# Top-32 attention and MLP-mixer: VectorE operations recast so that none reads two SBUF tiles in the tile loop, and the candidate chain interleaved

## The chip, the cores and the metric

The kernel runs on one core of one Trainium2 chip. The metric is the device time of one launch in microseconds; the median of the runs is compared. A profile is one execution recorded by the hardware profiler. In what follows VectorE is DVE in the profile's rows, ScalarE is ACT, GpSimd is POOL, TensorE is PE (its weight loads PEld), SyncE is SP.

## The reference

Attention over 8 batches and 8 heads, sequence 576, head width 64, where each query row keeps its 32 largest scores; the heads are concatenated and go through an MLP-mixer with a residual. In short:

```python
scores = scale * np.matmul(q, k.transpose(0, 1, 3, 2))          # 576 x 576 for each of 64 heads
kth = np.partition(scores, -32, axis=-1)[..., -32:-31]          # 32nd largest of each row
scores = np.where(scores >= kth, scores, -1e9)
attn = np.exp(scores - max); attn /= attn.sum + 1e-9
x = (attn @ v), heads side by side                              # 8 x 576 x 512
h = np.maximum(x.transpose(0, 2, 1) @ w_tok1, 0) @ w_tok2       # token mixing, 256 wide
u = x + h.transpose(0, 2, 1)
out = u + np.maximum(u @ w_ch1, 0) @ w_ch2                      # channel mixing, 1536 wide
```

## The kernel before

Two heads of one batch make a pair; there are 32 pairs. A pair's scores are cut into nine tiles of 128 query rows by 576 keys (four of each head, and one that holds the last 64 rows of both), 288 tiles in all. The loop bodies don't emit instructions: they add operations to a plan, each with an engine, an assumed duration and a due time (T is the assumed period of a tile), the operations it depends on, and the buffers it takes and uses. Plan.run then lists the operations engine by engine: at each step it takes the operation that could start first, and among those within 0.12 us of each other the one with the earlier due time. The instructions are emitted in that order, and each engine runs its own in that order.

A tile goes through these steps (tile_ops):

- TensorE multiplies q and k in float32 into PSUM, two tiles at a time (mm, L367; L359 for the ninth), in two of three "big" slots that the transposes of q and k and the MLP also use; ScalarE copies the scores into an Ssb buffer (L444) and takes exp of them into E, bfloat16 (L446).
- VectorE looks for a threshold near the 32nd largest score. The row's 576 scores are cut into seven segments and MAX8 gives each one's eight largest (L451), 56 candidates cd. Then MAX8 over the first two of each segment (L458); cut: scores at or above the eighth are set to zero by a scalar_tensor_tensor that reads cd twice (L461); MAX8 over the first five of each segment (L468); cut again (L461); MAX8 over all (L470), whose eighth value is th, of rank 24 to 31.
- ScalarE takes the sign of th - score (L472), bfloat16, and its row sum cnt, which tells th's rank. GpSimd multiplies scores and signs into X (L476), so that scores above the threshold become negative, and writes behind them seven dummies that are huge or hugely negative by cnt (L478). VectorE's MAX8 over X's 583 columns (L483) then has the 32nd largest score in place eight: m.
- VectorE writes the mask M = score >= m (L485); GpSimd multiplies E by M into Pm (L488) and copies th and m into thi and tlo for a test at the end (L491, L492).
- SyncE issues a DMA transpose of Pm into PT (L493). When a pair's nine are there, TensorE multiplies them by v and a column of ones (pv, L397), and VectorE divides by the sum on the way out of PSUM into Xb (L417 to L429).

When the four pairs of a batch are done, mlp_ops puts 33 groups of matmuls into the plan (TensorE L515 to L574, ScalarE L521 to L582), due over the next 36 tiles, and five stores. Behind the last tile VectorE tests that all thresholds were found (L604 to L619); a fallback that computes everything anew runs only if one wasn't.

Of the kernel before, what the change touches and what calls it, by code (L numbers as in the profile page):

```python
# [16 lines left out]
NDUM = 7  # L17


class Buf:  # L20
# [10 lines left out]
class Plan:  # L31
# [29 lines left out]
    def run(self):  # L61
# [15 lines left out]
        n = len(self.ops)  # L77
        while len(order) < n:
            best = None
            for eng, cs in cand.items():  # L80
                t0 = free[eng]
                pick = None
                early = None
                for o in cs:
                    r = o.ready if o.ready > o.due - self.AHEAD else o.due - self.AHEAD
                    ok = all(b.t is not None or b in o.acq for b in o.use)
                    taken = {}
                    for b in o.acq:
# [12 lines left out]
                    if early is None or r < early[0]:  # L101
                        early = key
                    if pick is None:
                        pick = (key, o)
                    else:
                        pr = pick[0][0]
                        if abs(r - pr) < 0.12:
                            if (o.due, o.n) < pick[0][1:]:
                                pick = (key, o)
                        elif r < pr:  # L110
                            pick = (key, o)
                if pick is not None and (best is None or pick[0][0] < best[0][0]):
                    best = pick
# [17 lines left out]
            done = o.end + o.lat  # L131
            if o.dma:
                dma_free = max(dma_free, o.end) + o.dma
                done = max(done, dma_free + 1.8)
# [6 lines left out]
                    s[1], s[2] = b.end, True  # L141
            for c in o.kids:
                c.wait -= 1
                t = done if (c.eng != o.eng or o.dma) else o.end
                if t > c.ready:
                    c.ready = t
                if c.wait == 0:
                    cand[c.eng].append(c)
# [7 lines left out]
def kernel(  # L156
# [23 lines left out]
    scale = 1.0 / float(D) ** 0.5  # L180
# [3 lines left out]
    ST = S - SM  # L184
    NPAIR = B * H // 2
    NT = NPAIR * 9
    XW = S + NDUM
    bounds = [round(i * S / NSEG) for i in range(NSEG + 1)]

    main = ExitStack()  # L190
# [3 lines left out]
    def sbt(name, shape, dt):  # L194
        return sb.tile(shape, dt, name=name, tag=name)
# [13 lines left out]
    kdum = sbt("kdum", [P, NDUM], f32)  # L209
    w1b = sbt("w1b", [P, 5, DT], bf16)  # L210
    w2b = sbt("w2b", [P, NJ, S], bf16)
    wc1b = sbt("wc1b", [P, NC, DC], bf16)
    wc2b = sbt("wc2b", [P, NF, C], bf16)
    cnt = sbt("cnt", [P, NT], f32)
    thi = sbt("thi", [P, NT], f32)
    tlo = sbt("tlo", [P, NT], f32)

    qLs = slots("qL", 3, [P, 5, 2, D], f32)
    slots("kL", 3, [P, 5, 2, D], f32)
    slots("vL", 2, [P, 5, 2, D], f32)  # L220
# [216 lines left out]

    def tile_ops(i, s, S_, om):

        E, cd, m8, th = Buf("E"), Buf("cd"), Buf("m8"), Buf("th")  # L440
        sg, X, M, Pm, PT = Buf("sg"), Buf("X"), Buf("M"), Buf("Pm"), Buf("PT")
        t = T * i

        ev = plan.add("ACT", 0.6, t + 0.6 * T, lambda: nc.scalar.copy(out=S_.t[:, :], in_=s.t[:, 0:S]),  # L444
                      [om], use=[s, S_])
        ex = plan.add("ACT", 0.6, t + 2.0 * T, lambda: nc.scalar.activation(  # L446
            out=E.t[:, :], in_=S_.t[:, :], func=AF.Exp, scale=scale), [ev], acq=[E], use=[S_])
        last = None
# [23 lines left out]
        ct = plan.add("ACT", 0.78, t + 2.2 * T, lambda: nc.scalar.activation(  # L472
            out=sg.t[:, :], in_=S_.t[:, :], func=AF.Sign, scale=-CUT, bias=th.t[:, 7:8],
            accum_out=cnt[:, i : i + 1]), [a5], acq=[sg], use=[S_, th])

        xm = plan.add("POOL", 1.4, t + 2.7 * T, lambda: nc.gpsimd.tensor_tensor(  # L476
            out=X.t[:, 0:S], in0=S_.t[:, :], in1=sg.t[:, :], op=ALU.mult), [ct], acq=[X], use=[S_, sg])
# [114 lines left out]
    for o in order:  # L592
# [204 lines left out]
```

## Time and profile before

| | |
|---|---|
| median of 2 runs | 1442.6 us (1441.63 to 1443.57) |
| the profiled execution's own time | 1438.56 us |
| its span | 1436.8 us |
| busy in the span: VectorE | 1281.4 us (89%) |
| TensorE matmul / weight loads | 893.9 us (62%) / 484.8 us (34%) |
| GpSimd | 907.7 us (63%) |
| ScalarE | 735.7 us (51%) |
| mean granted TensorE clock | 0.73 |

Busy time is the union of an engine's instructions over the span; the mean duration of one instruction stands in the groups of instructions; the timeline gives the start of each, in microseconds from the span's start, and merges neighbours of one kind (x7 is seven instructions, the time that of all). An engine's idle time before an instruction, and what ended it, stands behind it in brackets.

### The profile page before, as it was taken

What the parts mean: (1) busy time and instruction counts of PE and PEld (TensorE: products, weight loads), DVE (VectorE), ACT (ScalarE), POOL (GpSimd) and SP (SyncE); (2) the same over time, 40 slices, a digit from 0 to 9 for tenths busy, and PEclk for the clock granted to TensorE, in tenths of its full rate; (3) what the DMA queues carried; (4) which work ended last, traced back from release to release, by engine and by line L of the source; (5) the groups of instructions that cost most, each with busy time, mean ns of one, the idle gap of its engine ahead of it and who ended that gap; (6) DMA issues with size and microseconds to landing.
All of it is one profiled execution on the core that took longest, in us unless ns stands there. A gap on an engine that the chain in (4) does not pass through costs nothing. (4 is left out here: it accounts for less than half of the span.)

```text
span 1436.8 us, 18917 instructions
## 1 busy us (share of the span) xinstructions
PE 893.9 (62%) x4797; PEld 484.8 (34%) x4850; DVE 1281.4 (89%) x4256; ACT 735.7 (51%) x1465; POOL 907.7 (63%) x1451
## 2 busy tenths in 40 slices
PE   3645555875587665776567755687557656577437
PEld 2322323432343332433233322343224323333214
DVE  2999999999989999899999999899998999999960
ACT  2544446654466454654556544665446554565413
POOL 1756667666666666766676666766666666666640
PEclk9998557885578655976579855797558865698559
DMA  9422223332222322333223322333223332122111
GB/s 170 107 58 51 47 57 62 63 90 59 44 58 61 88 62 56 63 61 68 61 62 61 83 51 52 62 68 85 62 49 58 68 73 45 33 38 66 36 32 36
DMA packets 317190, 90.02 MB, mean 63 GB/s; under 512 B 309968, under 2 KB 311824, under 8 KB 317072
## 3 DMA queue, kind: packets, MB, share of 16 engines
q1 hardware_dynamic: 314496, 84.99, 28.8%
q0 software_dynamic: 2576, 3.74, 1.5%
q8 instruction: 40, 0.66, 0.2%
q14 instruction: 78, 0.64, 0.2%
HBM read 35.78 MB, written 9.44 MB: 31 GB/s over the span
## 5 line engine op out<-in xcount | busy, mean ns | idle before, releaser
L476 POOL TENSOR_TENSOR X<-Ssb,sg 128x576 f32<-128x576 f32 x288 | 369.2, 1282 | 268.9 <-DVE cd L451 135.5
L472 ACT ACTIVATE sg<-Ssb,th 128x576 bf16<-128x576 f32 x288 | 223.1, 775 | 577.3 <-DVE th L470 354.3
L488 POOL TENSOR_TENSOR Pm<-E,M 128x576 bf16<-128x576 bf16 x288 | 366.8, 1273 | 182.3 <-issue 163.5
L461 DVE SCALAR_TENSOR_TENSOR cd<-cd,m 128x14 f32<-128x14 f32 (+1 forms) x576 | 385.5, 669 | 19.6
L451 DVE MAX8 cd<-Ssb 128x8 f32<-128x82 f32 (+1 forms) x2016 | 321.7, 228 | 51.7 <-ACT Ssb L444 51.7
L367 PE MATMUL big<-kT,qT 64*128 64x512 f32 (+1 forms) x1024 | 303.4, 597 | 97.2 <-ACT Ssb L444 72.7
L397 PE MATMUL one<-vb,PT 128*128 128x65 bf16 (+2 forms) x1600 | 153.5, 228 | 221.6 <-DMA PT<-Pm 190.7
L367 PEld LDWEIGHTS big<-kT,qT 64*128 64x128 f32 x1024 | 148.9, 252 | 241.3 <-ACT Ssb L444 108.1
L483 DVE MAX8 m<-X 128x8 f32<-128x583 f32 x288 | 216.2, 751 | 3.6 <-POOL X L478 3.6
L485 DVE TENSOR_SCALAR M<-Ssb,m 128x576 bf16<-128x576 f32 x288 | 209.5, 728 | 8.6
L397 PEld LDWEIGHTS <-PT 128*128 128x128 bf16 (+2 forms) x1600 | 104.6, 113 | 269.7 <-DMA PT<-Pm 195.7
L446 ACT ACTIVATE E<-Ssb 128x576 bf16<-128x576 f32 x288 | 184.7, 682 | 1.7
L444 ACT COPY Ssb<-big 128x576 f32<-128x576 f32 x288 | 171.6, 630 | 9.4 <-PE big L367 5.0
L554 PE MATMUL big<-UT,wc1b 128*128 128x64 bf16 (+1 forms) x745 | 122.0, 316 | 79.8 <-ACT H L560 34.2
L569 PE MATMUL one<-wc2b,H 128*128 128x512 bf16 (+1 forms) x465 | 128.4, 422 | 21.8 <-DVE Xb L418 11.4
L478 POOL TENSOR_SCALAR X<-kdum,cnt 128x7 f32<-128x7 f32 x288 | 97.9, 340 | 27.4
L554 PEld LDWEIGHTS <-wc1b 128*128 128x128 bf16 x768 | 59.7, 107 | 140.8 <-issue 103.9
L569 PEld LDWEIGHTS <-H 128*128 128x128 bf16 (+1 forms) x480 | 50.6, 110 | 81.9 <-issue 33.6
L470 DVE MAX8 th<-cd 128x8 f32<-128x56 f32 x288 | 63.2, 220 | 9.7
L560 ACT ACTIVATE H<-big 128x576 bf16<-128x576 f32 x96 | 60.3, 643 | 18.3 <-PE big L554 17.9
L359 PE MATMUL big<-kT,qT 128*128 128x64 f32 (+1 forms) x128 | 59.2, 602 | 12.3 <-ACT kT L337 12.2
L468 DVE MAX8 m<-cd 128x8 f32<-128x35 f32 x288 | 57.1, 198 | 9.8
(67 smaller groups left out, 704.1 us busy)
## 6 DMA issues: line engine op xcount, KB each, us to landing
qL<-in_q_dram SPq DMA_DIRECT2D x64, 128.0 KB, 2.9
kL<-in_k_dram SPq DMA_DIRECT2D x64, 128.0 KB, 2.8
vL<-in_v_dram SPq DMA_DIRECT2D x64, 128.0 KB, 2.8
out_dram<-ob SPq DMA_DIRECT2D x32, 256.0 KB, 2.0
PT<-Pm SPq DMA_TRANSPOSE x288, 2.6
wc1b<-in_moe_w_ch_dram POOLq DMA_DIRECT2D x1, 1536.0 KB, 13.3
wc2b<-in_moe_w_ch_dram POOLq DMA_DIRECT2D x1, 1536.0 KB, 22.9
qL<-in_q_dram SPq DMA_DIRECT2D x64, 16.0 KB, 2.5
```

Source lines behind the costliest of these rows:

```text
L367: nc.tensor.matmul(out=bs[h].t[:, lo:hi], lhsT=qT.t[r, g * P : (g + 1) * P], rhs=kT.t[r, lo:hi], start=True, stop=True,)
L397: nc.tensor.matmul(out=o[0:m, g, :], lhsT=src[0:kr, j, cs], rhs=vb.t[0:kr, j, h, :], start=(j == 0), stop=(j == 4),)
L446: ex = plan.add("ACT", 0.6, t + 2.0 * T, lambda: nc.scalar.activation(out=E.t[:, :], in_=S_.t[:, :], func=AF.Exp, scale=scale), [ev], acq= ...
L451: segs.append(plan.add("DVE", 0.155, t + T + 0.01 * a, lambda a=a: nc.vector.max(cd.t[:, a, :], S_.t[:, bounds[a] : bounds[a + 1]]), [ev], ...
L461: return lambda: nc.vector.scalar_tensor_tensor(out=cd.t[:, :, 0:n], in0=cd.t[:, :, 0:n], scalar=m8.t[:, 7:8], in1=cd.t[:, :, 0:n], op0=AL ...
L472: ct = plan.add("ACT", 0.78, t + 2.2 * T, lambda: nc.scalar.activation(out=sg.t[:, :], in_=S_.t[:, :], func=AF.Sign, scale=-CUT, bias=th.t ...
L476: xm = plan.add("POOL", 1.4, t + 2.7 * T, lambda: nc.gpsimd.tensor_tensor(out=X.t[:, 0:S], in0=S_.t[:, :], in1=sg.t[:, :], op=ALU.mult), [ ...
L483: m = plan.add("DVE", 0.7, t + 3.4 * T, lambda: nc.vector.max(mx.t[:, :], X.t[:, 0:XW]), [dm], acq=[mx], use=[X])
L485: mk = plan.add("DVE", 0.4, t + 3.6 * T, lambda: nc.vector.tensor_scalar(out=M.t[:, :], in0=S_.t[:, :], scalar1=mx.t[:, 7:8], scalar2=None ...
L488: pm = plan.add("POOL", 1.4, t + 3.9 * T, lambda: nc.gpsimd.tensor_tensor(out=Pm.t[:, 0:S], in0=E.t[:, :], in1=M.t[:, :], op=ALU.mult), [m ...
L554: nc.tensor.matmul(out=pb.t[:, lo:hi], lhsT=wc1b[:, cc, fc * P : (fc + 1) * P], rhs=UT.t[:, cc, lo:hi], start=(cc == 0), stop=(cc == NC - 1))
L569: nc.tensor.matmul(out=pb.t[0:r, 0:C], lhsT=H2.t[:, fc, cs], rhs=wc2b[:, fc, :], start=(fc == 0), stop=False)
```

## The change

- The two cuts become match_replace: the eight values that MAX8 found are replaced by -1e30 in cd. Its operands are cd and the eight values.
- th and m are written straight into thi and tlo, which are now eight wide for each tile; GpSimd's two copies go.
- The dummies move from GpSimd to VectorE (a tensor_scalar of 3 rows of 3 columns at a pitch of 4, so nine dummies, in X's columns 576 to 587; the pad columns are set to a hugely negative value once). The long MAX8 reads 588 columns.
- The mask product has three forms, by the tile's place among nine. In six of nine ScalarE's exp goes into a "big" slot of PSUM, in float32, ordered behind X; VectorE does mask and product in one scalar_tensor_tensor that reads scores from SBUF and exp from PSUM. In two of nine VectorE negates the threshold (nt), and GpSimd makes the mask by two passes with one input (a huge multiple of the difference, clamped to 0 and 1) and multiplies. In one of nine GpSimd compares in one pass and multiplies.
- The plan: a VectorE result is ready for VectorE only 0.11 us after its operation; candidates for a start count as equal within 0.03 us in place of 0.12; the segments of a tile don't depend on each other any more; assumed durations and T (3.1 for 2.95) are new. Slots: kL 2 for 3, Ssb 8 for 6, PT 18 for 20, nt 4, Z 2, no th.

The diff, cut to its core:

```diff
@@ Plan.run
-                        if abs(r - pr) < 0.12:
+                        if abs(r - pr) < 0.03:
...
-                t = done if (c.eng != o.eng or o.dma) else o.end
+                t = done if (c.eng != o.eng or o.dma) else o.end + (0.11 if o.eng == "DVE" else 0.0)
@@ buffers
-    thi = sbt("thi", [P, NT], f32)
-    tlo = sbt("tlo", [P, NT], f32)
+    thi = sbt("thi", [P, NT, 8], f32)
+    tlo = sbt("tlo", [P, NT, 8], f32)
...
-    slots("kL", 3, [P, 5, 2, D], f32)
+    slots("kL", 2, [P, 5, 2, D], f32)
...
-    slots("Ssb", 6, [P, S], f32)
+    slots("Ssb", 8, [P, S], f32)
...
-    slots("PT", 20, [P, 5, P], bf16)
+    slots("PT", 18, [P, 5, P], bf16)
...
     for j in range(NDUM):
-        nc.vector.memset(kdum[:, j : j + 1], float(2 * (j + 1) - 529))
+        nc.vector.memset(kdum[:, j // 3, j % 3 : j % 3 + 1], float(2 * (j + 1) - 529))
+    for t in Xs:
+        nc.vector.memset(t[:, S:XW], -BIG)
...
-    T = 2.95
+    T = 3.1
@@ tile_ops
-        ex = plan.add("ACT", 0.6, t + 2.0 * T, lambda: nc.scalar.activation(
-            out=E.t[:, :], in_=S_.t[:, :], func=AF.Exp, scale=scale), [ev], acq=[E], use=[S_])
...
-            if a:
-                segs[a].deps.append(segs[a - 1])
...
         def cut(n):
-            return lambda: nc.vector.scalar_tensor_tensor(
-                out=cd.t[:, :, 0:n], in0=cd.t[:, :, 0:n], scalar=m8.t[:, 7:8], in1=cd.t[:, :, 0:n],
-                op0=ALU.is_lt, op1=ALU.mult)
+            return lambda: nc.vector.match_replace(cd.t[:, :, 0:n], m8.t[:, :], cd.t[:, :, 0:n], NEG)
...
-        a5 = plan.add("DVE", 0.14, tr + .04, lambda: nc.vector.max(th.t[:, :], cd.t[:, :, :]), [a4], acq=[th], use=[cd])
+        a5 = plan.add("DVE", 0.125, tr + .04, lambda: nc.vector.max(thi[:, i, :], cd.t[:, :, :]), [a4], use=[cd])
...
-        dm = plan.add("POOL", 0.15, t + 2.71 * T, lambda: nc.gpsimd.tensor_scalar(
-            out=X.t[:, S:XW], in0=kdum[:, :], scalar1=cnt[:, i : i + 1], scalar2=-BIG,
-            op0=ALU.add, op1=ALU.mult), [xm], use=[X])
-        mx = Buf("m8")
-
-        m = plan.add("DVE", 0.7, t + 3.4 * T, lambda: nc.vector.max(mx.t[:, :], X.t[:, 0:XW]), [dm], acq=[mx], use=[X])
-
-        mk = plan.add("DVE", 0.4, t + 3.6 * T, lambda: nc.vector.tensor_scalar(
-            out=M.t[:, :], in0=S_.t[:, :], scalar1=mx.t[:, 7:8], scalar2=None, op0=ALU.is_ge),
-            [m], acq=[M], use=[S_, mx])
-        pm = plan.add("POOL", 1.4, t + 3.9 * T, lambda: nc.gpsimd.tensor_tensor(
-            out=Pm.t[:, 0:S], in0=E.t[:, :], in1=M.t[:, :], op=ALU.mult), [mk, ex], acq=[Pm], use=[E, M])
-        kp = plan.add("POOL", 0.25, t + 3.95 * T, lambda: (
-            nc.gpsimd.tensor_copy(out=thi[:, i : i + 1], in_=th.t[:, 7:8]),
-            nc.gpsimd.tensor_copy(out=tlo[:, i : i + 1], in_=mx.t[:, 7:8])), [m], use=[th, mx])
+        dm = plan.add("DVE", 0.09, t + 3.3 * T, lambda: nc.vector.tensor_scalar(
+            out=X.t[:, S:XW].rearrange("p (a b) -> p a b", a=3)[:, :, 0:3], in0=kdum[:, :, 0:3],
+            scalar1=cnt[:, i : i + 1], scalar2=-BIG, op0=ALU.add, op1=ALU.mult), [ct, xm], use=[X])
+
+        m = plan.add("DVE", 0.68, t + 3.4 * T, lambda: nc.vector.max(tlo[:, i, :], X.t[:, 0:XW]), [dm, xm], use=[X])
+        thr = tlo[:, i, 7:8]
+        form = (0, 0, 1, 0, 0, 2, 0, 0, 1)[i % 9]
+        if form == 0:
+            Ep = Buf("big")
+            ex = plan.add("ACT", 0.6, t + 3.2 * T, lambda: nc.scalar.activation(
+                out=Ep.t[:, 0:S], in_=S_.t[:, :], func=AF.Exp, scale=scale), [ev, xm], acq=[Ep], use=[S_])
+            pm = plan.add("DVE", 0.7, t + 3.6 * T, lambda: nc.vector.scalar_tensor_tensor(
+                out=Pm.t[:, 0:S], in0=S_.t[:, :], scalar=thr, in1=Ep.t[:, 0:S], op0=ALU.is_ge, op1=ALU.mult),
+                [m, ex], acq=[Pm], use=[S_, Ep])
+        else:
+            ex = plan.add("ACT", 0.6, t + 2.4 * T, lambda: nc.scalar.activation(
+                out=E.t[:, :], in_=S_.t[:, :], func=AF.Exp, scale=scale), [ev], acq=[E], use=[S_])
+            if form == 1:
+                nt, Z = Buf("nt"), Buf("Z")
+                tn = plan.add("DVE", 0.07, t + 3.5 * T, lambda: nc.vector.tensor_scalar(
+                    out=nt.t[:, :], in0=thr, scalar1=-(1.0 - 2.0**-24), scalar2=None, op0=ALU.mult),
+                    [m], acq=[nt])
+                z = plan.add("POOL", 0.8, t + 3.7 * T, lambda: nc.gpsimd.tensor_scalar(
+                    out=Z.t[:, :], in0=S_.t[:, :], scalar1=nt.t[:, :], scalar2=BIG, op0=ALU.add, op1=ALU.mult),
+                    [tn], acq=[Z], use=[S_, nt])
+                mk = plan.add("POOL", 0.8, t + 3.71 * T, lambda: nc.gpsimd.tensor_scalar(
+                    out=M.t[:, :], in0=Z.t[:, :], scalar1=1.0, scalar2=0.0, op0=ALU.min, op1=ALU.max),
+                    [z], acq=[M], use=[Z])
+            else:
+                mk = plan.add("POOL", 2.0, t + 3.7 * T, lambda: nc.gpsimd.tensor_scalar(
+                    out=M.t[:, :], in0=S_.t[:, :], scalar1=thr, scalar2=None, op0=ALU.is_ge),
+                    [m], acq=[M], use=[S_])
+            pm = plan.add("POOL", 1.31, t + 3.9 * T, lambda: nc.gpsimd.tensor_tensor(
+                out=Pm.t[:, 0:S], in0=E.t[:, :], in1=M.t[:, :], op=ALU.mult), [mk, ex], acq=[Pm], use=[E, M])
```

## Rows read from the trace of the kernel before

**Rows 1.** The page: busy us, share of the span, instructions of each engine

```profile
PE 893.9 (62%) x4797; PEld 484.8 (34%) x4850; DVE 1281.4 (89%) x4256; ACT 735.7 (51%) x1465; POOL 907.7 (63%) x1451
```

**Rows 2.** VectorE's waits: waiter, releaser, us in total, times, longest

```profile
DVE cd L451 <- ACT Ssb L444: 51.7, 40, 26.2
DVE flag L619 <- PE one L618: 32.0, 1, 32.0
```

**Rows 3.** Timeline, VectorE, first and last tile: start, us, instruction, [idle before]

```profile
28.55 1.12 DVE L451 MAX8 cd<-Ssb 128x8 f32<-128x82 f32 x7 [26.18 <-ACT Ssb L444]
...
1370.97 0.23 DVE L451 MAX8 cd<-Ssb 128x8 f32<-128x82 f32 x1
```

**Rows 4.** Groups by shape, VectorE: busy us, mean ns, idle before

```profile
L451 DVE MAX8 cd<-Ssb 128x8 f32<-128x82 f32 x1440 | 282.1, 228 | 51.7 <-ACT Ssb L444 51.7
L461 DVE SCALAR_TENSOR_TENSOR cd<-cd,m 128x35 f32<-128x35 f32 x288 | 238.4, 828 | 10.1
L483 DVE MAX8 m<-X 128x8 f32<-128x583 f32 x288 | 216.2, 751 | 3.6 <-POOL X L478 3.6
L485 DVE TENSOR_SCALAR M<-Ssb,m 128x576 bf16<-128x576 f32 x288 | 209.5, 728 | 8.6
L461 DVE SCALAR_TENSOR_TENSOR cd<-cd,m 128x14 f32<-128x14 f32 x288 | 147.1, 511 | 9.5
...
L468 DVE MAX8 m<-cd 128x8 f32<-128x35 f32 x288 | 57.1, 198 | 9.8
L458 DVE MAX8 m<-cd 128x8 f32<-128x14 f32 x288 | 48.7, 169 | 4.4
L418 DVE TENSOR_TENSOR Xb<-one,rd 128x320 bf16<-128x320 f32 x32 | 15.7, 492 | 1.1
L425 DVE TENSOR_TENSOR Xb<-one,rd 128x256 bf16<-128x256 f32 x32 | 13.6, 425 | 0.0
```

**Rows 5.** Timeline from 28 to 35 us, VectorE and GpSimd, first two tiles

```profile
29.91 0.23 DVE L461 SCALAR_TENSOR_TENSOR cd<-cd,m 128x14 f32<-128x14 f32 x1
30.18 0.20 DVE L468 MAX8 m<-cd 128x8 f32<-128x35 f32 x1
30.42 0.26 DVE L461 SCALAR_TENSOR_TENSOR cd<-cd,m 128x35 f32<-128x35 f32 x1
...
30.84 1.10 DVE L451 MAX8 cd<-Ssb 128x8 f32<-128x82 f32 x7
...
31.91 1.28 POOL L476 TENSOR_TENSOR X<-Ssb,sg 128x576 f32<-128x576 f32 x1 [26.60 <-ACT sg L472]
...
32.19 1.02 DVE L461 SCALAR_TENSOR_TENSOR cd<-cd,m 128x14 f32<-128x14 f32 x1
```

**Rows 6.** Timeline near the last tiles: VectorE's mask M beside GpSimd

```profile
1376.31 0.52 DVE L485 TENSOR_SCALAR M<-Ssb,m 128x576 bf16<-128x576 f32 x1
...
1376.97 1.27 POOL L488 TENSOR_TENSOR Pm<-E,M 128x576 bf16<-128x576 bf16 x1 [1.28 <-issue]
1377.55 1.01 DVE L485 TENSOR_SCALAR M<-Ssb,m 128x576 bf16<-128x576 f32 x1
1378.19 0.41 POOL L491 COPY thi<-th 128x1 f32<-128x1 f32 x1
```

**Rows 7.** Groups by shape, GpSimd

```profile
L476 POOL TENSOR_TENSOR X<-Ssb,sg 128x576 f32<-128x576 f32 x288 | 369.2, 1282 | 268.9 <-DVE cd L451 135.5 <-ACT sg L472 130.9 <-DVE m L483 1.4
L488 POOL TENSOR_TENSOR Pm<-E,M 128x576 bf16<-128x576 bf16 x288 | 366.8, 1273 | 182.3 <-issue 163.5 <-POOL X L478 4.0
L478 POOL TENSOR_SCALAR X<-kdum,cnt 128x7 f32<-128x7 f32 x288 | 97.9, 340 | 27.4
...
L491 POOL COPY thi<-th 128x1 f32<-128x1 f32 x288 | 54.2, 188 | 0.0
```

**Rows 8.** Two stretches: us, each engine's busy us, granted TensorE clock, DMA

```profile
492.00:570.00 78.00, 42.80 (x181) 22.07 (x181) 74.66 (x247) 35.20 (x74) 51.45 (x83) 0.50 0.26 53
594.00:618.00 24.00, 16.61 (x137) 9.87 (x136) 21.49 (x73) 15.64 (x30) 15.25 (x25) 0.99 0.49 72
```

**Rows 9.** The page's groups: TensorE's score matmuls

```profile
L367 PE MATMUL big<-kT,qT 64*128 64x512 f32 (+1 forms) x1024 | 303.4, 597 | 97.2 <-ACT Ssb L444 72.7
```

**Rows 10.** Groups by shape, ScalarE: exp and score copies

```profile
L446 ACT ACTIVATE E<-Ssb 128x576 bf16<-128x576 f32 x288 | 184.7, 682 | 1.7
L444 ACT COPY Ssb<-big 128x576 f32<-128x576 f32 x288 | 171.6, 630 | 9.4 <-PE big L367 5.0 <-DVE M L485 4.1
```

More of the change, by code (lines that the diff above doesn't have):

```diff
@@ L16 @@
 RANK_BASE = 24
-NDUM = 7
+NDUM = 9
 class Buf:
@@ L186 @@
     NT = NPAIR * 9
-    XW = S + NDUM
+    XW = S + 12
     bounds = [round(i * S / NSEG) for i in range(NSEG + 1)]
@@ L208 @@
     identB = sbt("identB", [P, P], bf16)
-    kdum = sbt("kdum", [P, NDUM], f32)
+    kdum = sbt("kdum", [P, 3, 4], f32)
     w1b = sbt("w1b", [P, 5, DT], bf16)
@@ L227 @@
     slots("m8", 6, [P, 8], f32)
-    slots("th", 6, [P, 8], f32)
+    slots("nt", 4, [P, 1], f32)
+    slots("Z", 2, [P, S], f32)
     slots("sg", 3, [P, S], bf16)
-    slots("X", 4, [P, XW + 1], f32)
+    Xs = slots("X", 4, [P, XW], f32)
     slots("M", 4, [P, S], bf16)
     Ps = slots("Pm", 4, [P, 5 * P], bf16)
-    slots("PT", 20, [P, 5, P], bf16)
+    slots("PT", 18, [P, 5, P], bf16)
     slots("rd", 2, [P, 2, 5], f32)
@@ L438, in tile_ops @@
     def tile_ops(i, s, S_, om):
-        E, cd, m8, th = Buf("E"), Buf("cd"), Buf("m8"), Buf("th")
+        E, cd, m8 = Buf("E"), Buf("cd"), Buf("m8")
         sg, X, M, Pm, PT = Buf("sg"), Buf("X"), Buf("M"), Buf("Pm"), Buf("PT")
@@ L450, in tile_ops @@
         for a in range(NSEG):
-            segs.append(plan.add("DVE", 0.155, t + T + 0.01 * a, lambda a=a: nc.vector.max(
+            segs.append(plan.add("DVE", 0.146, t + T + 0.01 * a, lambda a=a: nc.vector.max(
                 cd.t[:, a, :], S_.t[:, bounds[a] : bounds[a + 1]]), [ev], acq=[cd] if a == 0 else [], use=[S_, cd]))
-            if a:
-                segs[a].deps.append(segs[a - 1])
         d = segs
@@ L460, in cut @@
         def cut(n):
-            return lambda: nc.vector.scalar_tensor_tensor(
-                out=cd.t[:, :, 0:n], in0=cd.t[:, :, 0:n], scalar=m8.t[:, 7:8], in1=cd.t[:, :, 0:n],
-                op0=ALU.is_lt, op1=ALU.mult)
+            return lambda: nc.vector.match_replace(cd.t[:, :, 0:n], m8.t[:, :], cd.t[:, :, 0:n], NEG)
         tr = t + 1.6 * T
-        a1 = plan.add("DVE", 0.1, tr, r1, d, acq=[m8], use=[cd])
-        a2 = plan.add("DVE", 0.1, tr + .01, cut(2), [a1], use=[cd, m8])
-        a3 = plan.add("DVE", 0.12, tr + .02, lambda: nc.vector.max(m8.t[:, :], cd.t[:, :, 0:5]), [a2], use=[cd, m8])
@@ L469, in tile_ops @@
-        a4 = plan.add("DVE", 0.12, tr + .03, cut(5), [a3], use=[cd, m8])
-        a5 = plan.add("DVE", 0.14, tr + .04, lambda: nc.vector.max(th.t[:, :], cd.t[:, :, :]), [a4], acq=[th], use=[cd])
[L472 to L476, printed above, removed]
-            out=X.t[:, 0:S], in0=S_.t[:, :], in1=sg.t[:, :], op=ALU.mult), [ct], acq=[X], use=[S_, sg])
@@ L488, in tile_ops @@
-        pm = plan.add("POOL", 1.4, t + 3.9 * T, lambda: nc.gpsimd.tensor_tensor(
-            out=Pm.t[:, 0:S], in0=E.t[:, :], in1=M.t[:, :], op=ALU.mult), [mk, ex], acq=[Pm], use=[E, M])
-        kp = plan.add("POOL", 0.25, t + 3.95 * T, lambda: (
-            nc.gpsimd.tensor_copy(out=thi[:, i : i + 1], in_=th.t[:, 7:8]),
-            nc.gpsimd.tensor_copy(out=tlo[:, i : i + 1], in_=mx.t[:, 7:8])), [m], use=[th, mx])
+        a1 = plan.add("DVE", 0.085, tr, r1, d, acq=[m8], use=[cd])
+        a2 = plan.add("DVE", 0.15, tr + .01, cut(2), [a1], use=[cd, m8])
@@ new lines, in tile_ops @@
+        a3 = plan.add("DVE", 0.1, tr + .02, lambda: nc.vector.max(m8.t[:, :], cd.t[:, :, 0:5]), [a2], use=[cd, m8])
+        a4 = plan.add("DVE", 0.17, tr + .03, cut(5), [a3], use=[cd, m8])
+        a5 = plan.add("DVE", 0.125, tr + .04, lambda: nc.vector.max(thi[:, i, :], cd.t[:, :, :]), [a4], use=[cd])
+        ct = plan.add("ACT", 0.77, t + 2.2 * T, lambda: nc.scalar.activation(
+            out=sg.t[:, :], in_=S_.t[:, :], func=AF.Sign, scale=-CUT, bias=thi[:, i, 7:8],
+            accum_out=cnt[:, i : i + 1]), [a5], acq=[sg], use=[S_])
@@ new lines, in tile_ops @@
+        xm = plan.add("POOL", 1.31, t + 2.7 * T, lambda: nc.gpsimd.tensor_tensor(
+            out=X.t[:, 0:S], in0=S_.t[:, :], in1=sg.t[:, :], op=ALU.mult), [ct], acq=[X], use=[S_, sg])
+        dm = plan.add("DVE", 0.09, t + 3.3 * T, lambda: nc.vector.tensor_scalar(
+            out=X.t[:, S:XW].rearrange("p (a b) -> p a b", a=3)[:, :, 0:3], in0=kdum[:, :, 0:3],
+            scalar1=cnt[:, i : i + 1], scalar2=-BIG, op0=ALU.add, op1=ALU.mult), [ct, xm], use=[X])
+        m = plan.add("DVE", 0.68, t + 3.4 * T, lambda: nc.vector.max(tlo[:, i, :], X.t[:, 0:XW]), [dm, xm], use=[X])
@@ L611 @@
     nc.vector.tensor_scalar(out=bad[:, 1:2], in0=bad[:, 1:2], scalar1=56.0, scalar2=None, op0=ALU.is_gt)
-    nc.vector.tensor_tensor(out=tmp[:, :], in0=thi[:, :], in1=tlo[:, :], op=ALU.is_gt)
-    nc.vector.scalar_tensor_tensor(out=tmp[:, :], in0=tlo[:, :], scalar=0.0, in1=tmp[:, :],
+    nc.vector.tensor_tensor(out=tmp[:, :], in0=thi[:, :, 7], in1=tlo[:, :, 7], op=ALU.is_gt)
+    nc.vector.scalar_tensor_tensor(out=tmp[:, :], in0=tlo[:, :, 7], scalar=0.0, in1=tmp[:, :],
                                    op0=ALU.is_gt, op1=ALU.mult)
```

## The prediction

> **What bounds the kernel now.** I read the page's busy line first. VectorE (DVE) is busy 1281.4 us of a span of 1436.8, far ahead of the others [rows 1]. Next its waits: its largest entry is 51.7 us for score copies on ScalarE, of which 26.2 us are the single wait before the first tile, and the next is 32.0 us for one matmul at the very end [rows 2]. So between head and tail VectorE waits about 25 us: it sets the pace. The first segment maximum starts at 28.55 us and that of the 288th tile at 1370.97 us [rows 3], which is (1370.97 - 28.55) / 287 = 4.68 us a tile, with a head of 28.6 us and 65.8 us from there to the span's end.
>
> Third, what VectorE does in 4.68 us. Two things in its groups of instructions [rows 4] don't fit their sizes: the two cuts of the candidates (L461) take 511 and 828 ns over 14 and 35 columns, while MAX8 over the same columns takes 169 and 198 ns. The timeline says why [rows 5]. With GpSimd idle the cuts took 0.23 and 0.26 us. The cut at 32.19 us took 1.02 us, and it ended at 33.21, just as GpSimd's product X, begun at 31.91, ended at 33.19: the cut, which reads SBUF twice, stood still until GpSimd was done. The mask M (L485), a tensor_scalar with one SBUF input, does it too: 0.52 us, but 1.01 us when begun inside GpSimd's Pm, and then GpSimd's small copy took 0.41 us in place of its mean of 0.19 [rows 6, 7].
>
> [...]
>
> One more reading: what an instruction costs depends on whether the next needs its result. Seven independent segment maxima of 228 ns each take 1.10 us together [rows 4, 5], so one starts every (1.10 - 0.228) / 6 = 0.145 us, 83 ns before the one ahead has ended. A dependent one starts 35 ns after the end (the cut at 29.91 ends at 30.14, L468 starts at 30.18; the difference of starts is 0.27). So an instruction's own cost is its duration less 0.083 us, and each exposed dependent link adds 0.118 us.
>
> **The change, part by part, per tile.**
>
> Removed: the two cuts, 0.511 - 0.083 = 0.43 and 0.828 - 0.083 = 0.745; the mask M on VectorE, 0.728 - 0.083 = 0.645 [rows 4]. Sum 1.82 us.
>
> Added: two match_replace. The trace has none. From below, one pass each at the price of MAX8 over the same columns: 0.169 - 0.083 = 0.086 and 0.115. From above, each is two instructions (load the eight values, replace) with an exposed link between: about 0.29 and 0.32, a second small instruction being 0.086 again. I take two instructions without the link, 0.17 and 0.20, since interleaving is what the new order works for: 0.37, bounds 0.20 and 0.61. The dummies (dm) come over from GpSimd: 9 columns, 0.08 to 0.09 by the 14-column row; its upper bound is rival A. The mask product pm runs on VectorE in 6 of 9 tiles, with one input in PSUM. Nearest are the normalizations, which also read PSUM: 492 ns for 320 columns, 425 for 256, so 1.05 ns a column [rows 4]; 576 columns make 0.76, less 0.083 is 0.675, times 6/9 is 0.45. The negated threshold tn (2 of 9 tiles): 0.02. Five more columns in the long MAX8: 0.005. Sum 0.93 us, so own costs fall by 0.89.
>
> Links: before, a tile's chain stands in a row, segments, r1, cut, maximum, cut, maximum, and m to M: six exposed links, 0.71 us. After, there are seven (dm to m comes in), but the order now charges 0.11 us for a VectorE result that VectorE uses and looks for other work meanwhile. Bounds: all hidden 0, all exposed 0.83. Seven segment maxima of the next tile and long MAX8s are there to fill with; I take one in four exposed, 0.21, a fall of 0.50.
>
> New period: 4.68 - 0.89 - 0.50 = 3.29 us.
>
> Does another engine reach that? GpSimd per nine tiles: nine X at 1.282 and three Pm at 1.273 are 15.4 us [rows 7], and five mask passes with one input. Those are not in the trace: from below 0.34 (7 columns), from above I take the two-input 1.27, as they read half as much; that gives 21.7 us, 2.4 a tile. They would have to average (29.6 - 15.4) / 5 = 2.8 us each to reach 3.29. dm and the two threshold copies leave GpSimd. ScalarE is busy 735.7 / 288 = 2.55 us a tile [rows 1] with the same passes as before, 78% of the new period. In front of exp on ScalarE there is now a wait for X on GpSimd and for a free PSUM slot in 6 of 9 tiles; score copies of later tiles queue behind it, and VectorE's segments wait for those. TensorE is the thin one: 893.9 / 8 = 112 us for each batch, and the new period gives a batch 36 x 3.29 = 118. [...] VectorE's roughly 25 us of waits in the body were with plenty of room; I take 45 us (bounds 0 and rival C).
>
> The rest costs nothing: one kL slot fewer (a load is needed every nine tiles, 30 us), two PT slots fewer (18 hold two whole pairs; the slots cover nine tiles each), wider thi and tlo, nine memsets in place of seven and four small ones more under the 26 us that VectorE waits at the start.
>
> Sum: 28.6 + 287 x 3.29 + 65.8 = 1039 us; plus 45, 1084 of span; the profiled execution lay 1.8 above its span and the median of the runs 4.0 above that execution (1442.6 and 1438.56), so about 1088.
>
> **The rivals.**
>
> A. The operations left on VectorE still wait for GpSimd. dm and tn are tensor_scalar with one SBUF input, as M was, and M waited [rows 6]. Against it: they are tiny, with 9 and 1 columns, and no row shows so small a one beside GpSimd. Price per waiting instruction between M's mean excess over its undisturbed time, 0.728 - 0.52 = 0.21, and the 35-column cut's, 0.828 - 0.26 = 0.57: say 0.39, times 288 dm and 64 tn, 137 us: 1225, between 1160 and 1290. The place is bad for it: dm becomes ready as X ends, when GpSimd takes its next pass.
>
> [...]
>
> B. The interleaving hides nothing: seven links exposed, 0.62 a tile more than I took: 1088 + 178 = 1266. For it: every link in the trace of before is exposed. Against: that order charged nothing for them.
>
> C. TensorE takes over. If its clock mix stays and it reaches some 85% busy, the body is 894 / 0.85 = 1052 us; with head and tail about 1145. For it: the margin of 112 to 118 us. Against: in the body VectorE waited for it hardly at all.
>
> D. Slower than before: PSUM. Three "big" slots serve score matmuls in pairs, transposes, the MLP and now exp. A pair's matmul holds two for 303.4 / 128 = 2.37 us, and the copies of 0.630 hold them on [rows 9, 10]: (2 x 2.37 + 3 x 0.63) / 2 = 3.3 slot-us a tile; 16 MLP groups and 8 transposes in 36 tiles, estimated at 2 us each, a little under a pair's matmul and copy, make 1.3; and exp and product hold one for 0.68 + 0.76 plus a wait w, in two tiles of three. With two of three slots usable at a time the period is (5.6 + 0.67 w) / 2, which passes the present 4.68 at w = 5.6 us; with 6.2 it is 4.88, and the time 1500. TensorE already waits 72.7 us for score copies [rows 9]. Against: exp is due 0.4 periods, 1.3 us, before its product, and waits for X first.
>
> **How the numbers follow.** Forecast 1088, chance 0.55, own range 1020 (all links hidden, fewer waits) to 1145. A 0.22 at 1225; C 0.12 at 1145; B 0.08 at 1266; D 0.03 at 1500. The range 1020 to 1245 leaves out B, D, the upper third of A and a small share below: about 2 in 10. Within 2% of 1442.6, about what a measurement of this kernel tells from no change, lies only the edge of D: faster 0.96, same 0.01, slower 0.03.
>
> **What would show it.** Right: the period between tiles' first segments near 3.3 us; VectorE still over 85% busy; match_replace near 0.2 to 0.3 us in each part with no second peak at 1.2; pm near 0.76 us; starts of dependent instructions with others between. A: dm's mean far above 0.15 us, ending where GpSimd's passes end. B: gaps of 35 ns all along the chain. C: VectorE's waits for score copies in the hundreds of us with TensorE over 85% busy. D: TensorE or exp waiting for slots that pm frees. Wrong on price: match_replace above 0.3 us a part, or GpSimd's mask passes near 2.8 us on average.

## The result and the profile after

| | before | after |
|---|---|---|
| median of 2 runs | 1442.6 us | 1093.2 us (1090.9 to 1095.4) |
| ratio | | 0.758, interval 0.751 to 0.765 |
| span of the profiled execution | 1436.8 us | 1089.2 us |
| one tile's period | 4.68 us | 3.48 us |

The forecast was 1088 us. The busy line of the page shows VectorE still far ahead, and GpSimd 272 us less busy than in [rows 1]:

```profile
PE 834.2 (77%) x4804; PEld 480.0 (44%) x4850; DVE 988.6 (91%) x5094; ACT 735.6 (68%) x1465; POOL 636.0 (58%) x555
```

The timeline of VectorE gives the period: the first and the 288th tile's first maximum over the candidates (L457) stand (1029.46 - 30.40) / 287 = 3.48 us apart (the segments, by which [rows 3] measured it, are now spread among other tiles' work).

```profile
30.40 0.15 DVE L457 MAX8 m<-cd 128x8 f32<-128x14 f32 x1
...
1029.46 0.17 DVE L457 MAX8 m<-cd 128x8 f32<-128x14 f32 x1
```

VectorE's waits, beside [rows 2]: of the 28.5 us for score copies 26.8 are the one wait before the first tile, and of the 12.1 us for the attention matmuls (L420) 6.3 come after the last. Between the two L457 above VectorE waits 11.0 us for other engines; between the same two places of the kernel before it was 25.5 us, all of it for score copies.

```profile
DVE flag L635 <- PE one L634: 31.7, 1, 31.7
DVE cd L452 <- ACT Ssb L447: 28.5, 4, 26.8
DVE rd L420 <- PE one L400: 12.1, 4, 6.3
```

Its groups by shape (busy us, mean ns, idle before), beside [rows 4]. L460 is match_replace, which is two instructions; L475 is dm, L486 the mask product with exp in PSUM:

```profile
L452 DVE MAX8 cd<-Ssb 128x8 f32<-128x82 f32 x1440 | 296.1, 229 | 28.6 <-ACT Ssb L447 28.5
L479 DVE MAX8 tlo<-X 128x8 f32<-128x588 f32 x288 | 222.1, 771 | 5.3 <-DVE m L457 0.4
L486 DVE SCALAR_TENSOR_TENSOR Pm<-Ssb,tlo,big 128x576 bf16<-128x576 f32 x192 | 155.7, 812 | 8.2 <-ACT big L484 0.8 <-DVE cd L460 0.4
...
L475 DVE TENSOR_SCALAR X<-kdum,cnt 128x9 f32<-128x9 f32 x288 | 125.6, 436 | 2.7 <-ACT sg L469 2.6
...
L460 DVE MATCH_REPLACE8 cd<-m,cd 128x35 f32<-128x35 f32 x288 | 51.9, 180 | 0.0
...
L460 DVE MATCH_REPLACE8 cd<-m,cd 128x14 f32<-128x14 f32 x288 | 45.3, 157 | 0.0
L460 DVE MATCH_VALUE_LOAD cd<-m,cd 128x8 f32 x576 | 42.8, 74 | 0.1
```

The cuts are cured: 157 and 180 ns, with 74 ns for each load in front, where they took 511 and 828. dm is not: 436 ns for nine columns. The timeline, VectorE beside GpSimd, shows a dm begun at 409.46 us, inside X, that ended at 410.59, as X ended at 410.57:

```profile
409.29 1.28 POOL L473 TENSOR_TENSOR X<-Ssb,sg 128x576 f32<-128x576 f32 x1 [2.00 <-ACT sg L469]
409.46 1.13 DVE L475 TENSOR_SCALAR X<-kdum,cnt 128x9 f32<-128x9 f32 x1
```

And the candidate chain on VectorE's timeline is no longer a chain; between nearly all of its links stands an instruction of another tile, here a segment, so that the chain's own links hardly cost a gap any more:

```profile
503.13 0.16 DVE L457 MAX8 m<-cd 128x8 f32<-128x14 f32 x1
503.20 0.23 DVE L452 MAX8 cd<-Ssb 128x8 f32<-128x83 f32 x1
503.35 0.07 DVE L460 MATCH_VALUE_LOAD cd<-m,cd 128x8 f32 x1
503.41 0.16 DVE L460 MATCH_REPLACE8 cd<-m,cd 128x14 f32<-128x14 f32 x1
503.48 0.23 DVE L452 MAX8 cd<-Ssb 128x8 f32<-128x82 f32 x1
503.63 0.18 DVE L465 MAX8 m<-cd 128x8 f32<-128x35 f32 x1
```

So the total came out as forecast, but by two misses of opposite sign: dm waits for GpSimd (rival A), and the 45 us set aside for other engines never fell due. The experiments take the parts apart. Behind each time stands, in brackets, its ratio to the kernel before, which was timed beside it (medians of 1443 to 1447 us), and the 95% interval of that ratio.

### The profile page after: what moved, and what is told of

Same layout as the page of the kernel before. It is cut to its first block, busy times and chain, and to the rows that moved or that the text cites. A ratio compares the mean times of both kernels' runs of the same rounds, so it can differ in the third digit from the quotient of the medians.

```text
span 1089.2 us, 19075 instructions
## 1 busy us (share of the span) xinstructions
PE 834.2 (77%) x4804; PEld 480.0 (44%) x4850; DVE 988.6 (91%) x5094; ACT 735.6 (68%) x1465; POOL 636.0 (58%) x555
## 5 line engine op out<-in xcount | busy, mean ns | idle before, releaser
L452 DVE MAX8 cd<-Ssb 128x8 f32<-128x82 f32 (+1 forms) x2016 | 382.0, 230 | 28.6 <-ACT Ssb L447 28.5
L469 ACT ACTIVATE sg<-Ssb,thi 128x576 bf16<-128x576 f32 x288 | 223.0, 774 | 209.9 <-DVE thi L467 170.7
L479 DVE MAX8 tlo<-X 128x8 f32<-128x588 f32 x288 | 222.1, 771 | 5.3 <-DVE m L457 0.4
L486 DVE SCALAR_TENSOR_TENSOR Pm<-Ssb,tlo,big 128x576 bf16<-128x576 f32 x192 | 155.7, 812 | 8.2 <-ACT big L484 0.8
L475 DVE TENSOR_SCALAR X<-kdum,cnt 128x9 f32<-128x9 f32 x288 | 125.6, 436 | 2.7 <-ACT sg L469 2.6
L507 POOL TENSOR_TENSOR Pm<-E,M 128x576 bf16<-128x576 bf16 x96 | 122.5, 1276 | 7.8
L484 ACT ACTIVATE big<-Ssb 128x576 f32<-128x576 f32 x192 | 124.2, 649 | 1.3 <-DVE Pm L486 1.0
L460 DVE MATCH_REPLACE8 cd<-m,cd 128x14 f32<-128x14 f32 (+1 forms) x576 | 97.1, 169 | 0.0
L497 POOL TENSOR_SCALAR Z<-Ssb,nt 128x576 f32<-128x576 f32 x64 | 47.8, 748 | 45.9 <-DVE nt L494 44.2
L490 ACT ACTIVATE E<-Ssb 128x576 bf16<-128x576 f32 x96 | 64.6, 677 | 0.9
```

What stands on the lines that cost most here:

```text
L452: segs.append(plan.add("DVE", 0.146, t + T + 0.01 * a, lambda a=a: nc.vector.max(cd.t[:, a, :], S_.t[:, bounds[a] : bounds[a + 1]]), [ev], ...
L469: ct = plan.add("ACT", 0.77, t + 2.2 * T, lambda: nc.scalar.activation(out=sg.t[:, :], in_=S_.t[:, :], func=AF.Sign, scale=-CUT, bias=thi[ ...
L475: dm = plan.add("DVE", 0.09, t + 3.3 * T, lambda: nc.vector.tensor_scalar(out=X.t[:, S:XW].rearrange("p (a b) -> p a b", a=3)[:, :, 0:3], ...
L479: m = plan.add("DVE", 0.68, t + 3.4 * T, lambda: nc.vector.max(tlo[:, i, :], X.t[:, 0:XW]), [dm, xm], use=[X])
L484: ex = plan.add("ACT", 0.6, t + 3.2 * T, lambda: nc.scalar.activation(out=Ep.t[:, 0:S], in_=S_.t[:, :], func=AF.Exp, scale=scale), [ev, xm ...
L486: pm = plan.add("DVE", 0.7, t + 3.6 * T, lambda: nc.vector.scalar_tensor_tensor(out=Pm.t[:, 0:S], in0=S_.t[:, :], scalar=thr, in1=Ep.t[:, ...
```

## Experiments on dm

**dm with unequal sizes.** Does dm's wait hang on the pattern it writes? In the kernel after, three rows of three go into three rows of three at a pitch of four; here the result is one run of nine. My guess was that it does.

```diff
-            out=X.t[:, S:XW].rearrange("p (a b) -> p a b", a=3)[:, :, 0:3], in0=kdum[:, :, 0:3],
+            out=X.t[:, S : S + 9].rearrange("p (a b) -> p a b", a=3), in0=kdum[:, :, 0:3],
```

> The kernel after, with one edit: the nine dummies are written to nine neighbouring columns, so that source and result of dm have outermost sizes 3 and 9 (odd and unequal) where they had 3 and 3. [...] Rival 1 (a tensor_scalar of this size waits for GpSimd whatever its pattern): mean still near 436 ns, time within 1% of 1093. Rival 2 (VectorE is no longer what sets the pace once dm is short, TensorE is): dm short, but the time above 1060 us, and VectorE's waits for score copies grow by tens of us.

Measured: 1039.1 us, ratio 0.717 (0.715 to 0.720). The group by shape and a dm inside X, from this kernel:

```profile
L475 DVE TENSOR_SCALAR X<-kdum,cnt 128x9 f32<-128x9 f32 x288 | 59.6, 207 | 4.9 <-ACT sg L469 4.9
```

```profile
419.76 1.28 POOL L473 TENSOR_TENSOR X<-Ssb,sg 128x576 f32<-128x576 f32 x1 [0.51 <-ACT sg L469]
419.88 0.21 DVE L475 TENSOR_SCALAR X<-kdum,cnt 128x9 f32<-128x9 f32 x1
```

The same operation on the same nine elements, begun inside X, now takes 0.21 us where the one above took 1.13. Only the pattern was changed. Two things of it changed together, the outermost size of the result (3 to 9) and the gaps between its rows (none now); no run tells them apart, and none shows why the pattern matters. The wait cost 1093 - 1039 = 54 us; of the 288 x (0.436 - 0.207) = 66 us that dm itself gave back, some 12 came back as waits for other engines, above all of the long MAX8 for X (7.2 us, where the kernel after shows none). Rivals 1 and 2 of this run fall: 1039 lies well below 1060, and VectorE's waits for score copies stay at 29.1 us, head included.

**dm back on GpSimd.**

```diff
-        dm = plan.add("DVE", 0.09, t + 3.3 * T, lambda: nc.vector.tensor_scalar(
+        dm = plan.add("POOL", 0.35, t + 2.71 * T, lambda: nc.gpsimd.tensor_scalar(
```

> The kernel after, with dm back on GpSimd behind X. VectorE loses 0.35 us a tile (dm's share of its starts in the kernel after), GpSimd gains about 0.35. If VectorE alone sets the pace: 1093 - 288 x 0.35 = about 993 us. If GpSimd's longer way from X to the long MAX8, or TensorE, is near the bound: over 1030 us, with VectorE waiting for X or for score copies by tens of us.

Measured: 1018.4 us (0.705, 0.703 to 0.706), between the two expectations and well below the kernel after: as it stood, the move of dm to VectorE lost 75 us. VectorE's busy share falls to 86%; its waits show where the rest of the 100 us went, exp in PSUM on ScalarE:

```profile
DVE Pm L486 <- ACT big L484: 29.2, 27, 3.6
```

## Experiments on the order, the cuts and the mask

**The old order, new operations.**

```diff
-                        if abs(r - pr) < 0.03:
+                        if abs(r - pr) < 0.12:
-                t = done if (...) else o.end + (0.11 if o.eng == "DVE" else 0.0)
+                t = done if (...) else o.end
+            if a:
+                segs[a].deps.append(segs[a - 1])
```

> The kernel after, with the order made as before: starts within 0.12 us count as equal, no 0.11 us for a VectorE result that VectorE uses, a tile's segments in a chain. Operations as after. Theory (each exposed dependent link costs 0.118 us, and the kernel after exposes less than one a tile): some six links come back, 0.6 us a tile, 170 us: about 1260 us. Rival (the order gains little, since a held instruction only uses up time that would be lost elsewhere): below 1150 us.

Measured: 1298.8 us (0.898, 0.896 to 0.899), so the order is worth 206 us in the kernel after, more than the 170 us expected of the links. Some 77 us of it stand at dm. Its mean rises from 436 ns to 513 (22 us): it now begins inside GpSimd's Pm in 79 tiles, where that was so in 8, and inside X in 49 in place of 66. The other 55 us are the link behind it:

```profile
503.04 0.92 DVE L477 TENSOR_SCALAR X<-kdum,cnt 128x9 f32<-128x9 f32 x1
504.06 0.78 DVE L481 MAX8 tlo<-X 128x8 f32<-128x588 f32 x1
```

Here, on the timeline of the kernel with the old order, the long MAX8 starts 0.10 us after dm has ended, at 503.96, where in the kernel after the instruction behind dm starts 0.09 us before dm's end. Link and wait add up.

**The old cuts, new order.**

```diff
-            return lambda: nc.vector.match_replace(cd.t[:, :, 0:n], m8.t[:, :], cd.t[:, :, 0:n], NEG)
+            return lambda: nc.vector.scalar_tensor_tensor(
+                out=cd.t[:, :, 0:n], in0=cd.t[:, :, 0:n], scalar=m8.t[:, 7:8], in1=cd.t[:, :, 0:n],
+                op0=ALU.is_lt, op1=ALU.mult)
```

> The kernel after, with the two cuts as scalar_tensor_tensor on two SBUF inputs again, order and all else as after (planned durations too). Theory (the wait for GpSimd is what the cuts cost): each cut again shows an undisturbed peak near 0.25 us and a tail to 1.3; the excess in the kernel before was 0.28 + 0.57 us a tile at GpSimd 63% busy, so at 58% about 0.78, times 288 = 225 us: about 1318 us. Rival (match_replace gained because two dependent links are hidden, the wait matters little): below 1180 us.

Measured: 1227.0 us (0.848, 0.846 to 0.849): 134 us slower than the kernel after, where 225 were expected. The groups:

```profile
L477 DVE TENSOR_SCALAR X<-kdum,cnt 128x9 f32<-128x9 f32 x288 | 163.0, 566 | 2.1 <-ACT sg L471 2.0
...
L460 DVE SCALAR_TENSOR_TENSOR cd<-cd,m 128x14 f32<-128x14 f32 x288 | 125.4, 436 | 0.1
L460 DVE SCALAR_TENSOR_TENSOR cd<-cd,m 128x35 f32<-128x35 f32 x288 | 112.2, 390 | 0.0
```

Over their undisturbed 0.23 and 0.26 us the cuts wait 0.21 + 0.13 = 0.34 us a tile, and dm waits 0.13 more; 0.47 x 288 = 135 us, which is the whole difference (without waits the cuts' own 0.15 + 0.18 us are about the 0.30 of the two match_replace). Scaling the waits of [rows 4] by GpSimd's busy share was wrong. Two cuts in a row waited more than these two, which stand apart: in the kernel before the second one began in the first 0.4 us of a GpSimd pass in 200 of 288 tiles, here in 90. That fits the means (828 ns in a row, 390 apart), but GpSimd was also less busy, 52% against 63%, and no run changes the place of the cuts alone. The run with the order alone, below, speaks for the place: 625 ns with GpSimd busier, at 73%.

**Either part alone on the kernel before.** First the cuts as match_replace, then only the order: the edits are those of the last two runs, the other way round.

> The kernel before with one edit: the two cuts as match_replace. In a chain without interleaving the pair cost 0.55 us a tile in the run with the old order, against 1.40 for the two cuts in the kernel before: 0.85 us less, 245 us, about 1198 us, if the waits vanish. Rival (GpSimd's passes come denser, and the mask M on VectorE takes over part of the waiting): M's mean grows from 728 ns toward 900, and the time is 1230 us or more.

Measured: 1216.4 us (0.844, 0.842 to 0.845), 18 us over the 1198 and below the rival's 1230. M on VectorE takes some of the waiting over, as the rival had it, but only a little: its mean goes from 728 to 764 ns, 10 us in all. The waits for score copies, 61.2 us for 51.7, are about the rest.

> The kernel before with the order alone as after (starts equal within 0.03 us, 0.11 us for a VectorE result that VectorE uses, segments free); operations as before. Theory (links and waits add up): some five of six exposed links go, 0.6 us a tile, 173 us, about 1270 us. Rival (the cuts still end when GpSimd's pass ends, so that time saved in front of a cut is waited out in it): above 1350 us, with the cuts' means larger than 511 and 828 ns.

Measured: 1276.3 us (0.886, 0.884 to 0.888), near the theory's 1270, though partly by another way. The cuts did not absorb the links' time; the second one, no longer right behind the first, even waits less, 625 ns for 828, which is 0.2 us a tile, 58 us in all or a third of the gain. The mask M in turn waits more, 826 ns for 728, 28 us in all. So the links are left with some 137 of the 167 us, where 173 were expected of them:

```profile
L483 DVE TENSOR_SCALAR M<-Ssb,m 128x576 bf16<-128x576 f32 x288 | 237.8, 826 | 1.1
...
L459 DVE SCALAR_TENSOR_TENSOR cd<-cd,m 128x35 f32<-128x35 f32 x288 | 179.5, 625 | 2.0
...
L459 DVE SCALAR_TENSOR_TENSOR cd<-cd,m 128x14 f32<-128x14 f32 x288 | 146.2, 508 | 0.6
```

Alone the two parts take 227 and 167 us from the kernel before.

**The mask as before, all else as after.** exp into E, M on VectorE, the product on GpSimd, in all tiles.

```diff
-        form = (0, 0, 1, 0, 0, 2, 0, 0, 1)[i % 9]
-        (the three forms)
+        mk = plan.add("DVE", 0.4, t + 3.6 * T, lambda: nc.vector.tensor_scalar(
+            out=M.t[:, :], in0=S_.t[:, :], scalar1=thr, scalar2=None, op0=ALU.is_ge),
+            [m], acq=[M], use=[S_])
```

> The kernel after, with the mask product as before in all tiles: exp into E in SBUF, M = score >= m on VectorE (tensor_scalar, one SBUF input), product on GpSimd. Order, match_replace and dm as after. VectorE loses pm's 0.49 us a tile and gains M: 0.44 undisturbed, 0.65 with the waits of the kernel before; dm waits more, since GpSimd's passes grow from 2.2 to 2.56 us a tile. Theory (the mask in PSUM pays by the waits it saves): 3.48 + 0.1 to 0.35 us a tile, 1125 to 1195 us, with M's mean near 0.73 us and dm's above 436 ns. Rival (exp in PSUM costs as much, since TensorE waits 46.5 us for slots that pm frees): 1093 us or less.

Measured: 1084.9 us (0.754, 0.751 to 0.756). Its interval overlaps that of the kernel after, so in the kernel after the mask's new forms brought nothing that can be measured. The groups show why:

```profile
L483 DVE TENSOR_SCALAR M<-Ssb,tlo 128x576 bf16<-128x576 f32 x288 | 235.6, 818 | 0.0
...
L475 DVE TENSOR_SCALAR X<-kdum,cnt 128x9 f32<-128x9 f32 x288 | 73.9, 257 | 0.5 <-ACT sg L469 0.5
```

M waits more than foreseen, 818 ns for 730, but dm all but ceases to: 257 ns in place of 436, or 0.18 us a tile, which I had expected to rise. So the theory's 1125 to 1195 us failed at dm. The time is the rival's, but not for its reason, slots of PSUM. On the timeline of this kernel dm falls where a pass of GpSimd ends:

```profile
501.92 1.28 POOL L486 TENSOR_TENSOR Pm<-E,M 128x576 bf16<-128x576 bf16 x1 [0.45 <-POOL X L473]
503.12 0.20 DVE L475 TENSOR_SCALAR X<-kdum,cnt 128x9 f32<-128x9 f32 x1
```

Pm ends at 503.20. In 202 of 288 tiles dm begins in the last 0.25 us of Pm in this way. What waits in this kernel is M, begun inside X in 260 tiles. To see whether the mask pays once dm does not wait, the same kernel with dm's sizes unequal:

> The kernel with the mask M on VectorE in all tiles (1085 us), and with dm's sizes odd and unequal, so that M is the only operation left on VectorE that waits for GpSimd. Theory (the exp in PSUM pays by M's waits, and the equal time of the two mask forms came from dm, which waited 0.17 us a tile with M on VectorE and 0.35 in the kernel after): dm falls from 0.174 to 0.125 us a tile, M keeps its 0.74, time about 1070 us, so that exp in PSUM is worth some 30 us against the 1039 us of the kernel that differs in the mask alone. Rival (waits move from one operation to the next, and the mask form is worth nothing): M's mean grows above 818 ns and the time stays at 1085 us, or it falls to 1045 us or less.

Measured: 1081.2 us (0.749, 0.748 to 0.750). It differs from the 1039.1 us kernel in the mask alone: with dm cured, the new forms are worth 42 us, more than the 30 expected. dm's cure, in turn, is worth 54 us with the new mask and 4 with the old one. The rival was half right: of the 0.055 us a tile that dm gave back (257 to 202 ns), M's mean took half, 818 to 844 ns.

## Experiments on the bounds

**All nine tiles with exp in PSUM** (rival D's mechanism, with dm's sizes unequal):

```diff
-        form = (0, 0, 1, 0, 0, 2, 0, 0, 1)[i % 9]
+        form = ((0,) * 9)[i % 9]
```

> The kernel with dm's sizes odd and unequal (1039 us), with exp in PSUM and the product on VectorE in all nine of nine tiles. VectorE gains three products of 0.73 in nine tiles less tn, 0.23 us a tile; GpSimd falls to 1.28 us a tile. If VectorE still sets the pace and PSUM slots suffice: 1039 + 66 = about 1105 us. If three slots are too few (the rival in which PSUM makes the kernel slow): above 1130 us, VectorE busy under 85%, and TensorE's waits for slots that pm frees grow from 32 us to over 100.

Measured: 1120.0 us (0.776, 0.775 to 0.777), 81 us over the 1039.1, where 66 were expected of VectorE's own work. TensorE does wait for slots that the product frees, 102 us, as D had it:

```profile
PE big L370 <- DVE Pm L486: 102.4, 75, 4.1
```

But VectorE stays at 89%, and its waits for exp are 21.6 us. By the expected 66 us PSUM is a tax of about 15 us here, not a bound.

**More tiles to GpSimd.** With dm's sizes unequal, four and five of nine in the two-pass form:

```diff
-        form = (0, 0, 1, 0, 0, 2, 0, 0, 1)[i % 9]
+        form = (0, 1, 0, 1, 0, 1, 0, 1, 0)[i % 9]      # then (0, 1, 0, 1, 0, 1, 1, 0, 1)
```

> The kernel with dm's sizes odd and unequal (1039 us), and with four of nine tiles instead of three given to GpSimd, all in the two-pass form. VectorE loses a mask product in one tile of nine (0.73 / 9 = 0.08 us a tile) less tn; GpSimd goes from 2.2 to (5 x 1.28 + 4 x 3.97) / 9 = 2.48 us a tile. If VectorE sets the pace: 3.30 - 0.07 = 3.23 us a tile, about 1018 us. If GpSimd's longer passes or TensorE stand in the way: 1035 us or more.

> The kernel with dm's sizes odd and unequal and four of nine tiles on GpSimd (1017 us), with five of nine. VectorE: 3.24 - 0.07 = 3.17 us a tile; GpSimd (4 x 1.28 + 5 x 3.97) / 9 = 2.77 us. If VectorE sets the pace: about 997 us. If GpSimd's passes, at 87% of the period and 4 us long in a row, now hold up X and with it the long MAX8: 1017 us or more, and VectorE's waits for X grow from 12.9 us.

Measured: 1016.7 us with four (0.705, 0.703 to 0.707), 1022.9 with five (0.708, 0.706 to 0.709). So a fifth tile brings nothing more, where 997 us had been expected. Four of nine and, of the runs above, dm on GpSimd (1018.4) are the fastest kernels, 7% below the kernel after. At five VectorE's busy share falls from 89% to 87%; but it is not X that it waits for, as I had written (8.9 us, fewer than the 12.9 with four); it is score copies and the attention matmuls, that is ScalarE and TensorE:

```profile
DVE cd L452 <- ACT Ssb L447: 39.8, 17, 26.7
DVE rd L420 <- PE one L400: 16.1, 14, 6.3
DVE rd L426 <- PE one L400: 9.5, 11, 1.8
```

## Why the prediction was right, and where it was not

The mechanism held for the cuts and the order: VectorE set the pace before and does after, the cuts' cost was waiting (match_replace alone takes 227 us from the kernel before), and the order hid most of the links. That the total came within 0.5% was luck. The sum, term by term, in us a tile:

| term | forecast | measured | from |
|---|---|---|---|
| two match_replace | 0.37 | 0.30 | 0.06 from each load to its pass, (0.157 - 0.083) and (0.180 - 0.083) for the passes |
| product with exp in PSUM, 6 of 9 | 0.45 | 0.49 | (0.812 - 0.083) x 6 / 9 |
| dm | 0.085 | 0.35 | 0.436 - 0.083 |
| exposed links | 0.21 | 0.13 | starts in the trace: 0.09 behind L457, 0.04 behind the first match_replace; it is nearly always the long MAX8 or the product that starts late there, not the next link of the chain |
| period | 3.29 | 3.48 | |
| waits for other engines in the body, over the whole | 45 us beside the 25.5 that 4.68 contains | 11.0 us in all | 5.8 for attention matmuls, 2.6 for signs, 1.8 for score copies, 0.8 for exp |

The period missed by 0.19 us a tile, 0.19 x 287 = 55 us. dm alone is 0.27 over and the product 0.04; match_replace is 0.07 under, and the waits for other engines fell by (25.5 - 11.0) / 287 = 0.05. The links fell by 0.49, almost the forecast 0.50: not from 0.71 but from 0.62, by the starts in the trace of before (not every link was exposed there, the one from the segments to the first maximum only in 129 of 288 tiles). dm is the step that failed: "its upper bound is rival A" was right, but I took the lower end. Of the 0.27, 0.04 is its own cost (207 ns undisturbed, not the 0.17 of the 14-column row) and 0.23 the wait. Rival A and its rows (M waits with one input) were the better forecast for dm, at 0.22 chance; its price was too high, 0.39 us for each where dm lost 0.436 - 0.207 = 0.23, since half of the 288 began while GpSimd was idle, and tn, priced with it, never waited (146 ns in the mean, 155 at most, though 28 of the 64 began inside a GpSimd pass).

The other miss hid the first. The 45 us stood for TensorE's thin margin, 112 us of work for each batch against 118, and they came on top of the 25 us of waits that the 4.68 us of before already contain. The kernel with dm's sizes unequal shows that they weren't owed even at the forecast's pace: its period is 3.30 us, it waits 23 us in the body, and its span is 1037.8 us, the sum without the 45 being 1039. From before to after TensorE's busy time fell from 893.9 to 834.2 us and its mean granted clock, a mix of the two levels of [rows 8], rose from 0.73 to 0.76; what moved the mix is not shown. The eight Ssb buffers may have helped: in the body the three kernels with six wait 25 to 34 us for score copies, those with eight 13 at most. But the slots and T were never changed alone, so this is not shown. 1084 + 55 - 45 - 4 (a head and tail of 90.1 us together for 94.4) is 1090, the span measured being 1089.2. Rival C did not come; with five of nine tiles on GpSimd VectorE waits 25.6 us for the attention matmuls, at most a beginning. Rival B is what the old order does to this kernel: 1299 us, where I had 1266.

One slip of the working changed little: the last sum, 1084 + 1.8 + 4.0, is 1090 and not 1088.

The forecast spoke of the mask product as a cost of 0.45 in place of 0.645, a fall of 0.2 us a tile. In the kernel after that fall was lost again: dm costs more in the company of the new forms, 0.35 against 0.17 us a tile. No term of the sum had this coupling.

## What to carry to other kernels

When one engine's short operations wait for another engine's long passes, count the operations that can wait, and cure all of them: with one left over, the others' cure can show up as its wait. Here the new mask forms and dm's cure together take 46 us from the kernel with neither (1084.9 to 1039.1), but the cure alone 4 us and the forms alone nothing. A small operation can sometimes be freed by its access pattern without moving it, as dm was (436 to 207 ns). And a sum that comes out right is no proof of its terms: here two misses of 55 and 45 us met.

## What the runs showed of the hardware that I had not expected

- Whether dm, a tensor_scalar of nine columns, waited for GpSimd's X hung on its shape: from 3 rows of 3 into 3 rows of 3 at a pitch of 4 it waited for the end of X (1.13 us above; 65 of the 66 begun inside X ended within 0.03 us of its end), from 3 rows of 3 into one run of 9 it did not (0.21 us above, 207 ns in the mean of 288). tn, of a single column, did not either (155 ns at most, 28 of its 64 begun inside X).
- GpSimd's compare of one input with a threshold (L504) took 1.73 us in the kernel after, where the clamp over as many elements (L500) took 0.67, and it did not hold dm all through: one begun 0.66 us into it ran its 0.21 us undisturbed:

```profile
L504 POOL TENSOR_SCALAR M<-Ssb,tlo 128x576 bf16<-128x576 f32 x32 | 55.3, 1727 | 8.9 <-DVE tlo L479 8.9
...
L500 POOL TENSOR_SCALAR M<-Z 128x576 bf16<-128x576 f32 x64 | 42.7, 667 | 5.6
```

```profile
401.54 1.73 POOL L504 TENSOR_SCALAR M<-Ssb,tlo 128x576 bf16<-128x576 f32 x1
...
402.20 0.21 DVE L475 TENSOR_SCALAR X<-kdum,cnt 128x9 f32<-128x9 f32 x1
```

  Of the 24 dm that began inside such a pass, seven began in its first 0.42 us and ended 0.76 to 0.77 us into it, 15 began 0.56 to 0.81 us into it and took 208 to 215 ns, and two began later than 1.1 us into it and ended 0.02 us after its end.
- In the kernel before, a segment maximum behind another started 0.083 us before its predecessor's end (the median), and a dependent instruction of the candidate chain 0.035 us after; with nothing but the order changed that was worth some 137 of the 167 us there. One short instruction in between did not always hide the link: in the kernel after, the long MAX8 stands behind another tile's L457 in 183 tiles, with its own dm just ahead of that, and in 180 of them it started about 0.02 us after the end of L457, which it does not read. Why is open.
